# Sinkhorn block attention with a residual MLP on one core: the first token half read from two PSUM tiles, row sums on ScalarE, and batches 2 and 3 mixed half a batch earlier

## The chip, the core and the metric

One core of one Trainium2 chip. The time is the device time in microseconds (us) of one launch: 275.54 us before the change, the median of three runs (274.01, 275.54, 275.88). The five engines that matter run their own instruction streams in order: TensorE (PE in the profile; its weight loads are PEld), VectorE (DVE), ScalarE (ACT), GpSimd (POOL) and SyncE (SP, which here only issues transfers). They meet through semaphores. TensorE accumulates in PSUM; the other operands lie in SBUF.

## What is computed

```python
# q, k, v: (4, 8, 768, 64); sort_net: (4, 8, 8, 8)
P = sort_net
for _ in range(5):                      # Sinkhorn
    P = exp(P - max(P, -1)); P = P / (sum(P, -1) + 1e-9); P = P / (sum(P, -2) + 1e-9)
k_sorted = einsum('bhij,bhjcd->bhicd', P, blocks(k))      # 8 blocks of 96 tokens
v_sorted = einsum('bhij,bhjcd->bhicd', P, blocks(v))
attn = softmax(blocks(q) @ k_sorted^T / 8)                # inside each block of 96
x = (attn @ v_sorted), heads side by side                 # (4, 768, 512)
a1 = alpha1 * x + beta1
u = x + lam * einsum('ts,bsd->btd', w_tok, a1)            # tokens mixed, 768 x 768
a2 = alpha2 * u + beta2
out = u + lam * (relu(a2 @ w_ch1) @ w_ch2)                # 512 -> 2048 -> 512
```

## The kernel before

The kernel works on four batches, each in two halves of 384 tokens. The MLP of a half is the frame: 16 `h_unit`s (four matmuls of 128x384 each, then a Relu on ACT from PSUM into `hTa` or `hTb`), then three token tiles `ch_unit`, each cut into four parts of four matmuls of 128x512. All else is hung between these units: `put(b, hf, kind, n, ...)` files work under a key and `run` emits it after unit n; kind "h" stands for the 16 h units and "c" for the 12 parts. Below, "(1,0) c4" is part 4 of half 0 of batch 1.

PE, DVE, ACT and POOL are wrapped in `Engine` (L55), whose `issue` (L65) keeps instructions in program order; so nearly every profile line says L65, and one has to read by tile names. SP is not wrapped: its transfers (L498, L552, L557, L670, L737, L738) go in an order that the tile scheduler chooses.

PSUM has two rings. `psa` has two buffers of two banks (scores `sc_ps`, attention output `x_ps`, key and value mixing `kmix_ps`, `mix_ps`); `psb` has four buffers of one bank (`h_ps`, `ch_ps`, `tok_ps`, and others). A new tile waits until whoever used that buffer last has been read out.

Batch 0 has a path of its own. k and v are sorted by small matmuls (`k_turn`, `v_mix`); `v_sort(n)` first copies a quarter of v into the layout `VD`, on ACT for n = 0 and 3 and on DVE for 1 and 2. `permute` and `wtok` bring w_tok into `w_tokT` by PE transposes. The first token half does not pass through DRAM: `first_tok(g)` (L616) puts the token product for 128 channels into `tok_ps`, and x transposed plus a rank-1 term (`brow`, `rrow`, the row sums of w_tok) into `turn_ps`; ACT copies the first, scaled, to `tok16`; `first_turn` (L632) adds `tok16` to `turn_ps` by one more matmul with the identity, and ACT makes `a2T` of it. The row sums come from six matmuls with a column of ones (`row_sums`, L586).

For a later batch b these steps run beside the MLP of batch b-1:

- `load_kv`, `load_q` (POOL queue, q0 in the profile): for b = 2 at (0,0) c11, for b = 3 at (1,0) c11.
- `mix_v(b, 0..2)`: three times two matmuls and a DVE copy into `mixed`; `bounce_v` and `back_v` (SP) send that through DRAM (`vscr`) into `Vs`, 96 x 64 rows of 64 half-floats. `mix_k`: three times eight matmuls, and four copies each into `kT`. All of these in half (b-1,0) for b = 2 and 3, from h8 on.
- `q_cross` (L495): six DMA transposes of q on SP, at (b-1,0) h11.
- `score` (8 matmuls, an exp on ACT) and `pv` (8 matmuls, reciprocal and product on DVE, and two more DVE operations, `first_affine`, filed in `late` until `flush`): 8 of each per batch, one per unit, from (b-1,0) c8 to (b-1,1) h11. `tails` then moves 32-row pieces.
- `moe_tok` for the first three token tiles, `moe_cross` (three DMA transposes of `u16` into `uT`, on SP, L670) at (b-1,1) c3, `moe_affine` (DVE makes `a2T` from `uT`) at c7. The first h unit of the next half needs that `a2T`.

```python
    def moe_cross(b, hf):
        uT = uT_of[(b, hf)] = att.tile([128, CT, 384], F16, name="uT", tag="uT", bufs=2)
        for m in range(3):
            nc.sync.dma_start_transpose(
                uT[:, :, m * 128:(m + 1) * 128], u16_of[b][:, 3 * hf + m, :],
            )
```

Of the kernel before, what the change touches and what calls it, by code (L numbers as in the profile page):

```python
# [16 lines left out]
def kernel(  # L17
# [58 lines left out]
    pool = Engine(nc.gpsimd)  # L76

# [83 lines left out]

    W1p = const([128, CT, HID], BF, "W1p")
# [8 lines left out]
    pool.dma_start(lamB[:], moe_lam.partition_broadcast(128))  # L171
    for g in range(4):
        pool.dma_start(W1p[:, :, g * 512:(g + 1) * 512], w1v[:, :, g * 512:(g + 1) * 512])
    brow = att.tile([1, C], F16, name="brow", tag="uT", bufs=2)
    rrow = att.tile([1, 384], F16, name="rrow", tag="uT", bufs=2)
    ones16 = const([128, 1], F16, "ones16")
    pool.memset(ones16[:], 1.0)
# [76 lines left out]
    def v_sort(n, eng):  # L254
        eng(
            VD[:, n * 16:(n + 1) * 16, 0:HB],
            v8[:, :, n * 16:(n + 1) * 16].rearrange("p t d -> p d t"),
        )

# [8 lines left out]
    def q_out(g):  # L268
# [8 lines left out]
        4: [lambda: q_out(1), lambda: q_out(2), lambda: q_out(3), lambda: warm(5)],  # L277
# [155 lines left out]
    def pv_first(g):  # L433
        if g == 0:
            x_of[0] = moep.tile([128, 8, C], F16, name="x128", tag="x128", bufs=2)
            a1_of[0] = moep.tile([128, 8, C], F16, name="a1", tag="a1", bufs=1)
        ps = psa([128, 2, 512], FT, "x_ps")[:, :, 0:480].rearrange("p a (k d) -> p a k d", d=80)
        for i in range(NB):
            for h2 in range(2):
                et = ets[(0, g, i // 4)][:].rearrange("p a i t -> p (a i t)")  # L440
                lo = (4 * h2 + i % 4) * BLK
                w = min(128, 8 * BLK - lo)
                val = Vs[0][:, (2 * g + h2) * NB + i, 0:D + 1]
                if i < 6:
                    pe.matmul(ps[0:w, h2, i, 0:D + 1], et[:, lo:lo + w], val, start=True, stop=True)
                else:
                    for a in range(3):
                        pe.matmul(
                            ps[96:128, h2, 3 * (i - 6) + a, 0:D + 1], et[:, lo + a * 32:lo + (a + 1) * 32], val,
                            start=True, stop=True,  # L450
                        )
        rc = att.tile([128, 2, 6], FT, name="rc", tag="rc", bufs=3)
        dve.reciprocal(rc[:], ps[:, :, :, D])
        dve.tensor_tensor(
            x_of[0][:, 0:NT, g * 128:(g + 1) * 128].rearrange("p k (a d) -> p k a d", a=2),
            ps[:, :, :, 0:D].rearrange("p a k d -> p k a d"),
            rc[:].rearrange("p a k -> p k a").unsqueeze(3).to_broadcast([128, NT, 2, D]), ALU.mult,
        )

    def pv(b, g, hf):  # L460
# [20 lines left out]
        flush()  # L481
# [4 lines left out]
    def flush():  # L486
        while late:
            late.pop()()
# [6 lines left out]
    def q_cross(b, kt):  # L495
        if kt == 0:
            qT_of[b] = att.tile([128, H4, S], F16, name="qT", tag="qT", bufs=1)
        nc.sync.dma_start_transpose(  # L498
# [51 lines left out]
    def bounce_v(b):  # L550
        for th in range(2):
            nc.sync.dma_start(  # L552
                vscr[b, :, th * HB:(th + 1) * HB, :], mixed[b][th * 64:(th + 1) * 64, :, :],
            )

    def back_v(b):
        nc.sync.dma_start(Vs[b % 2][0:BLK, :, 0:D], vscr[b].rearrange("x t d -> t x d"))  # L557
# [4 lines left out]
    def permute(half, eng):  # L562
        wp = wp_of[half] = (moep, att)[half].tile(
            [128, 3, NT, 128], F16, name="wp", tag=("u16", "raw")[half], bufs=(1, 2)[half]
        )
        src = wt16[half]
        eng(wp[:, :, :, 0:96], src[:, :, 0:TAIL].rearrange("p m (k c) -> p m k c", c=96))
        eng(wp[:, :, :, 96:128], src[:, :, TAIL:S].rearrange("p m (k c) -> p m k c", c=32))
# [7 lines left out]
    ab2col = const([128, 4 * CT], FT, "ab2col")  # L576

    def prep_ab2(ps):
        tps = ps([128, 4 * CT], FT, "ab2_ps")
        pe.transpose(tps[:], ab2[:], ident16f[:])  # L580
        act.copy(ab2col[:], tps[:])
        dve.tensor_tensor(
            ab2col[:, 3 * CT:4 * CT], ab2col[:, 2 * CT:3 * CT], ab2col[:, 3 * CT:4 * CT], ALU.mult
        )

    def row_sums(ps):  # L586
        ps = ps([1, 384], FT, "rr_ps")
        for ks in range(NT):
            pe.matmul(ps[:], ones16[:], w_tokT[:, ks, 0:384], start=(ks == 0), stop=(ks == NT - 1))
# [26 lines left out]
    def first_tok(g):  # L616
        c = slice(g * 128, (g + 1) * 128)
        tps, ups = (psb([128, 384], FT, n)[:] for n in ("tok_ps", "turn_ps"))
        for ks in range(NT):
            pe.matmul(  # L620
                tps, x_of[0][:, ks, c], w_tokT[:, ks, 0:384], start=(ks == 0), stop=(ks == NT - 1),
            )
        for m in range(3):
            pe.matmul(
                ups[:, m * 128:(m + 1) * 128], x_of[0][:, m, c], ident16[:],
                start=(m == 0), stop=True, skip_group_check=True,
            )
        pe.matmul(ups, brow[:, c], rrow[:], start=False, stop=True, skip_group_check=True)
        act.activation(tok16[:, g, :], tps, AF.Copy, scale=ab2col[:, 3 * CT + g:3 * CT + g + 1])
        return ups  # L630

    def first_turn(g, ups, eng):  # L632
        pe.matmul(ups, ident16[:], tok16[:, g, :], start=False, stop=True, skip_group_check=True)
        affine(0, 0, g, ups, eng)
# [32 lines left out]
    def moe_cross(b, hf):  # L667
        uT = uT_of[(b, hf)] = att.tile([128, CT, 384], F16, name="uT", tag="uT", bufs=2)
        for m in range(3):
            nc.sync.dma_start_transpose(  # L670
# [31 lines left out]
    def last_out(hT, cps, kk, kt):  # L702
        for n in range(2):
# [11 lines left out]
            nc.sync.dma_start(out[B - 1, kt * 96:(kt + 1) * 96, c], ost[0:96, :])  # L715
# [25 lines left out]
    act_out = nc.sync.dma_start  # L741
# [7 lines left out]
    warm(4)  # L749
    kp0 = k_turn(0, 0, psb)  # L750
# [3 lines left out]
    warm(1)  # L754
# [6 lines left out]
    mix_values(0, psb)  # L761
    k_copy(0, 3, kp3, 0, copy)
    k_copy(0, 3, kp3, 1, act.copy)
    v_sort(0, act.copy)
    v_sort(1, copy)
    score(0, 0, 0, psa)
    score(0, 0, 1, psa)
    warm(3, psb)
    v_mix(0, 0, psb, copy)
    v_mix(0, 1, psb, copy)  # L770
    v_sort(2, copy)
# [3 lines left out]
    v_sort(3, act.copy)  # L775
# [8 lines left out]
    permute(0, copy)  # L784
# [3 lines left out]
    wtok(0, act.copy)  # L788
    wtok(1, act.copy)
    wtok(2, act.copy)  # L790
    score(0, 3, 0, psa)
    pv_first(1)
    wtok(3, act.copy)
    wtok(4, act.copy)
    wtok(5, act.copy)
    score(0, 3, 1, psa)
    permute(1, copy)
    row_sums(psb)
    prep_ab2(psb)
    t0 = first_tok(0)  # L800
    pv_first(2)
    first_turn(0, t0, act)
    t1 = first_tok(1)
    pv_first(3)
    first_turn(1, t1, act)
    t2 = first_tok(2)
    first_turn(2, t2, act)
    t3 = first_tok(3)

# [16 lines left out]
    for ks in range(NT):  # L826
        put(0, 0, "h", ks, lambda ks=ks: prep_wtok(ks, 1, psb, (dve.tensor_copy, act.copy)[ks % 2]))
    for n in range(1, B):
        put(max(n - 2, 0), n > 1, *(("h", 10), ("c", 9))[n > 1], lambda n=n: mix_matrix(n))
# [5 lines left out]
    put(0, 0, "c", 3, lambda: moe_affine(0, 1))  # L835
    for b in range(1, B):
        p = b - 1
        off = 3 if b == 1 else 0
        for n in range(3):
            put(p, 0, "h", (13 if b == 1 else 8) + n, lambda b=b, n=n: mix_v(b, n, dve.tensor_copy))  # L840
        put(p, 0, "h", 15 if b == 1 else 10, lambda b=b: bounce_v(b))
        put(p, 0, "c", 4 if b == 1 else 0, lambda b=b: back_v(b))
        for n in range(3):
            put(
                p, 0, *(("c", 3 + 3 * n) if b == 1 else (("h", 15), ("c", 1), ("c", 4))[n]),
                lambda b=b, n=n: mix_k(b, n, ((act.copy, dve.tensor_copy)[(n + (b > 1)) % 2],) * 4),
            )
        for kt in range(NT if b > 1 else 0):
            put(p, 0, "h", 11, lambda b=b, kt=kt: q_cross(b, kt))
        for g in range(0 if b > 1 else H4):  # L850
            put(p, 0, "c", off + (1, 4, 7, 7)[g], lambda b=b, g=g: q_turn_late(b, g, (dve.tensor_copy, act.copy, dve.tensor_copy, act.copy)[g]))
        if b + 1 < B:
            put(p, 0, "c", 11, lambda b=b: load_kv(b + 1), lambda b=b: load_q(b + 1))
        seq = [("s", 0), ("s", 1), ("s", 2), ("p", 0), ("s", 3), ("p", 1), ("p", 2), ("s", 4), ("p", 3), ("s", 5),
               ("p", 4), ("s", 6), ("p", 5), ("s", 7), ("p", 6), ("p", 7)]
        if b == 1:
            when = [("h", 0), ("h", 1), ("h", 2), ("h", 3), ("h", 4), ("h", 5), ("h", 6), ("h", 7), ("h", 8), ("h", 9),
                    ("h", 10), ("h", 11), ("h", 12), ("h", 13), ("h", 14), ("h", 15)]
        else:
            when = [("c", 8), ("c", 9), ("c", 10), ("c", 10), ("c", 11), ("c", 11), ("h", 0), ("h", 1), ("h", 2), ("h", 3),  # L860
                    ("h", 4), ("h", 5), ("h", 6), ("h", 8), ("h", 9), ("h", 11)]
        for (kind, n), (ph, at_) in zip(seq, when):
            f = (lambda b=b, n=n: score(b, n // 2, n % 2, psa)) if kind == "s" else (lambda b=b, n=n: pv(b, n // 2, n % 2))
            put(p, 1 if ph == "h" else 0, ph, at_, f)
        last = [("h", 12), ("h", 15)][b == 1]
        put(
            p, 1, *last, lambda b=b: tails(a1_of[b], 0, C, dve.tensor_copy),
# [3 lines left out]
        for kt in range(3):  # L871
            put(p, 1, "c", 4 if b == 1 else 3, lambda b=b, kt=kt: moe_tok(b, kt, psb))
        put(p, 1, "c", 4 if b == 1 else 3, lambda b=b: moe_cross(b, 0))
        put(p, 1, "c", 8 if b == 1 else 7, lambda b=b: moe_affine(b, 0))
# [5 lines left out]
    for ci in range(2):  # L880
        for m in range(3):
            h_part(0, 0, m, [ci])
    first_turn(3, t3, act)
    for m in range(3):
        h_part(0, 0, m, [2])
# [44 lines left out]
```

## Time and profile before

The profiled execution took 275.76 us, of which the span on the core is 274.0 us; that is 0.22 us over the median of the three timed runs.

| engine | busy us | share of span | instructions |
|---|---|---|---|
| PE | 260.2 | 95% | 2159 |
| DVE | 169.7 | 62% | 351 |
| ACT | 117.1 | 43% | 219 |
| POOL | 96.4 | 35% | 104 |

The stages follow from the first `h_ps` matmul of each half in the timeline of PE. (0,0) begins at 39.58 us, (0,1) at 72.59, (1,0) at 103.24, (1,1) at 132.94, (2,0) at 163.93, (2,1) at 195.32, (3,0) at 223.76 and (3,1) at 248.40. Half (3,1) holds the MLP alone; (3,0) holds the MLP and 18 token matmuls in 24.64 us.

How to read it: spans of PE overlap, since matmuls are pipelined, so the cost of a group is the distance from its start to the next start. Four h matmuls take 0.65 us in this sense, four `ch_ps` matmuls 0.87, six `tok_ps` matmuls 1.29. The releaser named after an idle time is the one that came last. DMA share over 1 means that packets overlap.

### The profile page before, as it was taken

The numbers are of one execution on the slowest core, as the hardware profiler recorded it, in microseconds if no ns is written. First come the engines' busy times: TensorE is split into PE (matmuls) and PEld (weight loads), VectorE is DVE, ScalarE is ACT, GpSimd is POOL, SyncE is SP. The second block draws the span as 40 slices with busy tenths as digits, with TensorE's granted clock in tenths as the row PEclk, the third lists the DMA queues.
The fourth block names the chain that finished last, engine by engine and source line by source line (L and its number), as shares of the span: only waits on it lengthen the run. The fifth ranks groups of instructions, "written<-read, shape, count | busy, mean of one in ns | idle before, by whom it ended". The sixth has DMA issues, their size and how long they took to land.

```text
span 274.0 us, 5366 instructions
## 1 busy us (share of the span) xinstructions
PE 260.2 (95%) x2159; PEld 140.4 (51%) x2173; DVE 169.7 (62%) x351; ACT 117.1 (43%) x219; POOL 96.4 (35%) x104
## 2 busy tenths in 40 slices
PE   7998899999999999999999969999999999999993
PEld 3466555455556444554455424564465445545552
DVE  5787527896468978576778725586689755121032
ACT  2588547234787002553674002554674004604600
POOL 8647102701472094403560824402200746122000
PEclk9999999999999999999999997999999999999999
DMA  6999999998989942249399952149300223012012
GB/s 103 211 206 193 206 207 214 173 115 178 128 176 175 133 116 78 59 115 145 86 182 165 113 138 61 38 118 117 106 10 2 76 58 77 22 38 77 0 41 77
DMA packets 67372, 31.04 MB, mean 113 GB/s; under 512 B 56642, under 2 KB 63058, under 8 KB 67348
## 3 DMA queue, kind: packets, MB, share of 16 engines
q0 software_dynamic: 26352, 15.34, 40.1%
q1 hardware_dynamic: 40900, 15.30, 30.9%
q8 instruction: 17, 0.28, 0.4%
q14 instruction: 7, 0.06, 0.1%
q10 hardware_dynamic: 96, 0.07, 0.1%
HBM read 32.79 MB, written 8.65 MB: 151 GB/s over the span
## 4 chain that ended last, share of the span: by engine, by line
PE 77%; DVE 9%; DMA 6%; issue 3%; SPq 2%; ACT 2%; POOL 0%; DVEq 0%; POOLq 0%
PE h_ps L65 30%; PE ch_ps L65 21%; PE tok_ps L65 10%; PE x_ps L65 3%; DMA out_dram<-ost 2%; PE sc_ps L65 2%; DVE ost L65 2%; DVE a L65 2%; DVE x L65 2%; PE warm_ps L65 2%; DMA q<-in_q_dram 2%; DMA uT<-u 2%; PE mix_ps L65 1%; PE kmix_ps L65 1%; SPq L737 1%
## 5 line engine op out<-in xcount | busy, mean ns | idle before, releaser
L65 PE MATMUL h_ps<-a2T,W1p 128*128 128x384 bf16 x512 | 97.2, 328 | 2.4 <-DVE a2T L65 2.1
L65 ACT ACTIVATE hTa<-h_ps 128x384 bf16<-128x384 f32 x96 | 47.0, 492 | 95.3 <-PE h_ps L65 95.1
L65 PE MATMUL ch_ps<-W2p,hTa 128*128 128x512 bf16 (+1 forms) x287 | 67.3, 370 | 0.6
L65 POOL TENSOR_TENSOR ost<-ost,u 128x512 f32<-128x512 f32 x21 | 26.6, 1267 | 116.1 <-DVE ost L65 110.0
L65 PEld LDWEIGHTS <-W1p 128*128 128x128 bf16 x512 | 47.6, 99 | 35.3 <-issue 5.0
L65 PEld LDWEIGHTS <-hTa 128*128 128x128 bf16 x300 | 28.4, 98 | 29.0
L65 DVE TENSOR_TENSOR ost<-ch_ps,lamB 128x512 f32<-128x512 f32 (+1 forms) x25 | 16.7, 670 | 37.9 <-PE ch_ps L65 34.6
L65 POOL TENSOR_TENSOR u<-toktmp,x 128x512 f32<-128x512 f32 x18 | 29.2, 1635 | 6.7 <-DVE toktmp L65 6.6
L65 PE MATMUL tok_ps<-a,w_tokT 128*128 128x512 f16 x126 | 30.5, 386 | 0.0
L65 ACT ACTIVATE et<-sc_ps 96x768 f16<-96x768 f32 (+1 forms) x32 | 25.6, 812 | 10.8 <-PE sc_ps L65 10.8
L65 PE MATMUL ch_ps<-W2p,hTb 128*128 128x512 bf16 (+1 forms) x99 | 24.8, 370 | 0.1
L65 DVE TENSOR_TENSOR toktmp<-tok_ps,lamB 128x512 f32<-128x512 f32 x21 | 14.4, 687 | 11.8 <-PE tok_ps L65 10.5
L65 PEld LDWEIGHTS <-w_tokT 128*128 128x128 f16 x126 | 12.3, 99 | 14.5 <-issue 1.1
L65 DVE TENSOR_TENSOR u<-toktmp,x 128x512 f16<-128x512 f32 (+1 forms) x24 | 18.9, 800 | 0.7
L65 ACT ACTIVATE hTb<-h_ps 128x384 bf16<-128x384 f32 x32 | 15.7, 490 | 8.0 <-PE h_ps L65 7.6
L65 POOL DMA_DIRECT2D qn<-in_q_dram x18 | 16.0, 924 | 4.7 <-DMA raw<-in_v_dram 4.7
L65 DVE CAST kT<-kmix_ps 64x512 f16<-64x512 f32 x20 | 14.2, 712 | 4.5 <-PE kmix_ps L65 3.0
L65 DVE TENSOR_TENSOR x<-x_ps,rcb 96x512 f16<-96x512 f32 x24 | 16.5, 686 | 0.8
L65 PE MATMUL x_ps<-Vs,et 96*128 96x65 f16 (+4 forms) x288 | 14.4, 195 | 2.3 <-DVE x L65 1.1
L65 DVE TENSOR_SCALAR a2T<-uT,ab2col 128x384 bf16<-128x384 f16 x28 | 10.6, 440 | 9.3 <-DMA uT<-u 9.3
L65 PEld LDWEIGHTS <-et 96*128 96x128 f16 (+4 forms) x288 | 12.4, 100 | 7.2 <-DVE x L65 2.3
L65 ACT CAST kT<-kmix_ps 64x512 f16<-64x512 f32 x16 | 11.5, 716 | 9.8 <-PE kmix_ps L65 9.6
(113 smaller groups left out, 237.8 us busy)
## 6 DMA issues: line engine op xcount, KB each, us to landing
out_dram<-ost SPq DMA_DIRECT2D x23, 192.0 KB, 2.4
raw<-in_v_dram POOLq DMA_DIRECT2D x6, 384.0 KB, 8.1
raw<-in_k_dram POOLq DMA_DIRECT2D x6, 384.0 KB, 10.0
qn<-in_q_dram POOLq DMA_DIRECT2D x18, 128.0 KB, 10.3
vscr<-mixed SPq DMA_DIRECT2D x6, 384.0 KB, 3.6
Vs<-vscr SPq DMA_DIRECT2D x3, 768.0 KB, 8.0
W1p<-in_moe_w_ch_dram POOLq DMA_DIRECT2D x4, 512.0 KB, 13.0
W2p<-in_moe_w_ch_dram POOLq DMA_DIRECT2D x4, 512.0 KB, 17.3
```

Source lines behind the costliest of these rows:

```text
L65: ins = getattr(self.eng, name)(*args, **kwargs)
L737: act_out(out[b, kt * 96:(kt + 1) * 96, :], ost[0:96, :])
```

## The change

- SP is wrapped too: all transfers on it go in program order.
- The first token half keeps its two PSUM tiles apart. `first_turn` has ACT write alpha2 * (x transposed + rank 1) + beta2 into a new tile `z`; `first_mm` makes `tok_ps`; `first_finish` has DVE compute `a2T = tok_ps * scale + z` in one operation. The identity matmul goes. `tok16` is still copied by ACT. The fourth group is moved behind the first three h matmuls.
- The row sums of w_tok come from ACT (`row_sum`, a copy with `accum_out`, three of 128x768), then three narrow PE transposes.
- `v_sort`: 0 and 1 on DVE, 2 on ACT, 3 on POOL, ahead of the four W1 loads in its queue. `mix_values(0)` is put ahead of `k_turn`. The two small `ab2col` steps go earlier, `permute` is cut, and four of the six first `wtok` copies go from ACT to DVE.
- For b = 2 and 3, `mix_v`, `bounce_v`, `q_cross` and `mix_k` move from half (b-1,0) to the c stage of half (b-2,1), with all copies on ACT; `back_v` goes to (b-1,0) h6; the loads of batch 3 go from (1,0) c11 to (1,0) h6.
- For b = 2 and 3 scores and pv go in pairs, at (b-1,0) h15, c1, c3, c6, c8, c11 and (b-1,1) h1, h4; `flush` is put one unit after each pair of pv. `tails` goes from h12 to h8, the three first `moe_tok` from c3 to c0, c1, c2, `moe_cross` from c3 to c2, `moe_affine` from c7 to c6.

```diff
+    sp = Engine(nc.sync)
...
+    v_sort(3, pool.tensor_copy)
     for g in range(4):
         pool.dma_start(W1p[:, :, g * 512:(g + 1) * 512], w1v[:, :, g * 512:(g + 1) * 512])
...
+    def row_sum(m):
+        if m == 0:
+            a1_of[0] = moep.tile([128, 8, C], F16, name="a1", tag="a1", bufs=1)
+        act.activation(a1_of[0][:].rearrange("p k c -> p (k c)")[:, 0:S], wt16[0][:, m, :], AF.Copy, accum_out=rcol[:, m:m + 1])
...
     def row_sums(ps):
-        ps = ps([1, 384], FT, "rr_ps")
-        for ks in range(NT):
-            pe.matmul(ps[:], ones16[:], w_tokT[:, ks, 0:384], start=(ks == 0), stop=(ks == NT - 1))
+        rc16 = const([128, 3], F16, "rc16")
+        act.copy(rc16[:], rcol[:])
+        ps = ps([1, 384], F16, "rr_ps")
+        for m in range(3):
+            pe.transpose(ps[:, m * 128:(m + 1) * 128], rc16[:, m:m + 1], ident16[:])
         act.copy(rrow[:], ps[:])
...
+    def first_finish(g):
+        dve.scalar_tensor_tensor(
+            a2T_of[0][0][:, g, :], tps_of[g], ab2col[:, 4 * CT + g:4 * CT + g + 1], z_of[0][:, g, :],
+            op0=ALU.mult, op1=ALU.add,
+        )
+        if g == 3:
+            tok_copy(g)
...
-    def first_turn(g, ups, eng):
-        pe.matmul(ups, ident16[:], tok16[:, g, :], start=False, stop=True, skip_group_check=True)
-        affine(0, 0, g, ups, eng)
+        act.activation(
+            z_of[0][:, g, :], ups, AF.Identity, bias=ab2col[:, CT + g:CT + g + 1], scale=ab2col[:, g:g + 1],
+        )
...
+        else:
+            for n in range(3):
+                put(p - 1, 1, "c", 4 + n, lambda b=b, n=n: mix_v(b, n, act.copy))
+                put(p - 1, 1, "c", 7 + 2 * n, lambda b=b, n=n: mix_k(b, n, (act.copy,) * 4))
+            put(p - 1, 1, "c", 7, lambda b=b: bounce_v(b))
+            put(p, 0, "h", 6, lambda b=b: back_v(b))
+            for kt in range(NT):
+                put(p - 1, 1, "c", 6 + kt, lambda b=b, kt=kt: q_cross(b, kt))
+            if b + 1 < B:
+                put(p, 0, "h", 6, lambda b=b: load_kv(b + 1), lambda b=b: load_q(b + 1))
+            for (kind, n), at_ in zip(
+                pairs, ((0, "h", 15), (0, "c", 1), (0, "c", 3), (0, "c", 6), (0, "c", 8), (0, "c", 11), (1, "h", 1), (1, "h", 4)),
+            ):
+                if kind == "p":
+                    put(p, at_[0], at_[1], at_[2] + 1, flush)
+                for i in range(2):
+                    f = (lambda b=b, n=n + i: score(b, n // 2, n % 2, psa)) if kind == "s" else (lambda b=b, n=n + i: pv(b, n // 2, n % 2))
+                    put(p, *at_, f)
...
-            put(p, 1, "c", 4 if b == 1 else 3, lambda b=b, kt=kt: moe_tok(b, kt, psb))
-        put(p, 1, "c", 4 if b == 1 else 3, lambda b=b: moe_cross(b, 0))
-        put(p, 1, "c", 8 if b == 1 else 7, lambda b=b: moe_affine(b, 0))
+            put(p, 1, "c", 4 if b == 1 else kt, lambda b=b, kt=kt: moe_tok(b, kt, psb))
+        put(p, 1, "c", 4 if b == 1 else 2, lambda b=b: moe_cross(b, 0))
+        put(p, 1, "c", 8 if b == 1 else 6, lambda b=b: moe_affine(b, 0))
...
-    for ci in range(2):
+    for m in range(3):
+        h_part(0, 0, m, [0])
+    first_turn(3, psa)
+    first_mm(3, psa)
+    for ci in (1, 2):
         for m in range(3):
             h_part(0, 0, m, [ci])
```

Here `pairs` is `[("s", 0), ("s", 2), ("p", 0), ("s", 4), ("p", 2), ("s", 6), ("p", 4), ("p", 6)]`; `p` is b-1.

## The prediction

> **What bounds the kernel now.** I read the page's engine shares and slices first, then PE by half, then the chain around the one half that is too long, then the queues that feed it.
>
> ```profile
> PE   7998899999999999999999969999999999999993
> ...
> PEclk9999999999999999999999997999999999999999
> ```
>
> ```profile
> 24.14:41.65 17.51, 15.89 (x192) 10.25 (x193) 7.42 (x13) 9.98 (x19) 3.84 (x6) 1.00 1.24 207
> ...
> 72.59:103.24 30.65, 30.41 (x258) 15.66 (x259) 22.75 (x49) 13.84 (x26) 15.84 (x16) 1.00 1.07 145
> 103.24:132.94 29.70, 29.50 (x206) 15.60 (x208) 20.11 (x36) 13.27 (x24) 8.69 (x6) 1.00 0.61 103
> 132.94:163.93 30.99, 28.25 (x215) 14.66 (x213) 21.56 (x47) 10.83 (x21) 15.94 (x16) 1.00 1.04 136
> 163.93:195.32 31.39, 31.19 (x206) 16.09 (x208) 19.72 (x36) 13.27 (x24) 8.77 (x6) 0.95 0.54 93
> 195.32:223.76 28.44, 27.85 (x215) 14.66 (x213) 23.14 (x49) 10.83 (x21) 8.56 (x6) 1.00 0.14 37
> ```
>
> PE is full in nearly every slice: it is the bound, and only PE work removed or PE stalls closed can shorten the span. The windows (length, then busy us of PE, PEld, DVE, ACT, POOL, then clock, DMA share and GB/s) show where PE is not full: 1.6 us before the first h units, 2.7 us in (1,1); and (2,0) ran at a granted clock of 0.95. The chain of waits there:
>
> ```profile
> 158.93 0.83 SPq L670
> ...
> 161.16 2.32 DMA uT<-u
> ...
> 163.50 0.39 DVE a2T L65
> ...
> 163.93 1.19 PE h_ps L65 x4
> 165.13 2.11 PE tok_ps L65 x6
> 167.23 2.17 PE h_ps L65 x8
> ```
>
> PE waits 2.05 us for `a2T`, that for `uT`, that for SP. Then the next groups are slow: 1.19, 2.27 and 2.38 us in the timeline where 0.81, 1.46 and 1.46 are usual, 2.1 us lost, at a granted clock of 0.60 from 164.8 to 168.2. The SP queue says why `uT` was late, and two more rows price what the change moves:
>
> ```profile
> 122.45 0.34 SPq L557 DMA_DIRECT2D Vs<-vscr  x1
> ...
> 148.86 8.20 SPq L498 DMA_TRANSPOSE qT<-qn  x6
> ...
> 158.25 4.13 SPq L670 DMA_TRANSPOSE uT<-u  x3
> ```
>
> ```profile
> 137.34 0.34 PE L65 MATMUL sc_ps<-qT,kT 64*128 64x96 f16 x8
> 137.62 0.82 PE L65 MATMUL h_ps<-a2T,W1p 128*128 128x384 bf16 x4
> 138.28 0.42 PE L65 MATMUL x_ps<-Vs,et 96*128 96x65 f16 x8
> 138.54 0.82 PE L65 MATMUL h_ps<-a2T,W1p 128*128 128x384 bf16 x4
> ```
>
> Six q transposes hold SP from 148.86 to 157.16, an output and then `uT` follow. From starts: a score costs 0.28 us, a pv 0.26; but from an h start to the next score is 0.75 and to the next pv 0.66, so a switch into scores costs about 0.10 more.
>
> **The change up to the first h units, before 41.65 us.** There the fourth weight slice of h units 0 to 2 begins. PE loses four identity matmuls (0.17 each, 0.66) and six row-sum matmuls (29.70 to 30.76, 1.06, less some 0.25 for three narrow transposes): 1.5 us in all. Following each engine in order with these rows: VD waits for DVE now, whose three `bigV` steps (0.22 each) and two small ones push the k copies back by 0.75, so v_mix starts at about 18.1 as before; its seventh copy is ACT's, so attention output begins at 24.0 (was 24.14). v_sort(3) on POOL is not in the trace: between 0.4 (its 256-element copy) and 1.5 us (ACT's); even 3 us would end by 20, v_mix needs it at 22. It holds up W1 (issued 16.8, landing 13 us later, needed at 39.6): hidden by 10 us. From 24.0: x_ps and scores as before, DVE takes four w_tokT copies (0.36) and two halves of `permute` (1.4), so the third x is ready at 32.3, the fourth at 34.7; the token product 0 ends at 31, 2 at 35; the fourth after the first h slice, at 37.4; its `first_finish`, priced at 0.6 by the 512-wide product from PSUM (0.69) and bounded by 0.44 and 0.96, at 38.15; slice four begins at 38.4. The three ACT row sums cost 0.8 each by the exp of the same width; at 1.5 (the strided copy) `rrow` is 1.5 us late and the first turn waits for it. So 41.65 becomes 38.4, or 39.9: gain 3.25, at worst 1.7. The later (0,0) has one 0.13 matmul more (`mix_matrix(2)`): gain 3.1. Its loads stay ahead: queue q0 finishes q of batch 1 at 57, needed at 64.
>
> **The halves from 72.59 to 223.76.** These last 151.2 us. What PE has to do there, from starts: MLP 20.76 (16 x 0.65 + 12 x 0.865) and tokens 3.88 in each of five halves; mixing 2.65 (3 x 0.43 + 3 x 0.45). After the change:
>
> - (0,1): 30.65, less 0.13 and the 0.25 wait, and 2.65 of mixing: 32.9.
> - (1,0): 24.64, four score pairs (2 x 0.27 + 0.10 = 0.64, so 2.56), four pv (1.04), 0.13: 28.4.
> - (1,1): 24.64, four pv, 2.65: 28.3. (2,0): 28.2. (2,1): 25.7.
>
> Sum 143.5: 7.7 us less. Of these 4.2 are the wait at 163.93 and its clock, 0.8 the pairs, about 1.1 two waits for DVE's x (136.33, 198.61), the rest smaller waits. This holds if `uT` comes in time: three tokens at c0 to c2, the last u16 about 8.2 us into the stage, `uT` 2.5 us later, DVE 1.25: ready at 12; the stage runs for 17. q's transposes now stand behind `uT` on SP.
>
> What is added against that:
>
> 1. *ACT's queue.* Each mix_k costs ACT four copies, 2.9 us; three are issued within 4.4 us, so 8.7 us of copies reach past the stage. The end of the third is some 4.4 us into the next half. Behind it on ACT are the Relus; `psb` has four buffers, so the second token group (PE ready 3.25 us in) waits for the first Relu at 4.8. PE waits 1.6 us at (1,0) and at (2,0): 3.2. Below, 0, if the third mix_k gets its copies sooner than these rows say; above, what rival B adds.
> 2. *Vs.* back_v stands on SP behind the three `uT` of (b-1,0) h4. From the end of the third token group T: product 0.96, u16 0.73, transpose 1.2, so it is issued at T + 2.95 and lands 8.0 later (all three landings took 8.0): T + 11.0. The first pv pair needs it after 11 h units, two score pairs and four ch parts: T + 11.9. For batch 3 that is enough. For batch 2 POOL issues the loads of batch 3 at about T + 2.6 to 4.7, on the same 16 engines. No row shows the two together. Vs is 6144 packets of 128 B, which filled 122.5 to 129.0; k and v are 256 packets of 6144 B at 474 ns, and q 6144 small ones. Below: nothing lost. Above: Vs moves one small packet per big one, gets through only after k and v (8 us) and then shares with q: 11.5 us of waiting. I take the time shared equally: in the row of batch 2's load only 39 of 256 packets moved in the first 3 us, so Vs, which moved 1710 in its first 1.5 us alone, gets about 2900 out early; the other 3200, 3.3 us alone, take 6.6, then 1.5 to be seen: T + 13.9, PE waits 2.0 us. Behind it on PE stands everything. A clock drop after it costs 0 (waits of 0.59 and 0.81 had none) to 1.7 (after 2.05): as 2.0 stands at the edge, 0.85.
>
> The Trainium skill ("DMA: Bandwidth & Descriptors", section on queues, rings and completion order) says that an engine takes rows in turn by the packet, some 9 to 17 descriptors at a time. By that rule, an estimate, sixteen small ones (0.27 us) would alternate with a 0.47 us one, Vs would come some 5 us late, and with a clock drop the sum be about 274.7. No run here shows it yet.
>
> SP's order otherwise: outputs of c7 now stand between q's first transpose and the rest; `ost` has two buffers, so a late output stops DVE only a tile later, and none is that late by my count: 0.
>
> Sum: -3.1 - 7.65 + 3.2 + 2.0 + 0.85 = -4.7. Against the profiled 275.76 that is 271.06; the profiled run was 0.22 above the median, so 270.8.
>
> **Rivals.**
>
> A. *Vs behind the loads*, at the first pv pair of (1,0). For: back_v and the loads are issued within half a microsecond, and the margin is 0.9. Against: Vs starts first. Without any Vs term the sum is 268.0; a wait of 6 to 11.5 us and a clock drop of 1.7 give 275.7 to 281.2. From a wait of 8.6 us on it is over 1% slower.
>
> B. *ACT becomes the bound at two h starts*, with a clock drop each: 3.4 more, 274.2. For: ACT gets 12 copies and 3 more per batch. Against: 1.6 us is less than the 2.05 that had a drop.
>
> C. *The front does not get shorter*: DVE (34.7 for the last x) or ACT takes the place of PE, or POOL's copy is several us. 273.9.
>
> D. Nothing of the Vs and ACT waits appears: 264.8.
>
> **How the numbers follow.** The forecast with its near cases (267 to 273, D included) has 0.64; A 0.18, B 0.09, C 0.09. 1% (272.8 to 278.3) is about what a measurement can tell here. Faster: 0.61 of the forecast, 0.04 of B and C: 0.65. Slower: half of A and a little: 0.10. Same: 0.25. Range: from 265.5, near D, to 276.5, which leaves out most of A. The forecast's own range is 267 to 273.
>
> **What would show it.** First h slice four at 38.4 (C: over 41). No `h_ps <- DVE a2T` wait and a PEclk without the dip at 164. Stage lengths as listed. PE waiting for ACT at the second token group of (1,0) and (2,0), under 2 us each. At the first pv of (1,0), PE waiting for DMA Vs: about 2 us, in A over 6, with Vs landing in 15 us or more while q0 moves big packets. Wrong would be: pairs that wait for their exps in the c stage (I count 0.3 us of slack), an SP queue where `uT` is late behind an output, or DVE's flushes coming before an `ost` that PE needs.

## The result, and the profile after

The changed kernel takes 285.29 us (median of four runs, 284.43 to 285.87) where the kernel before, run beside it, takes 274.77 (273.17 to 275.88): a ratio of 1.0385, 95% interval 1.0317 to 1.0453. It is slower, and outside the range that was given. The profiled execution took 284.78 us, its span is 283.0.

Two rows of the page of the changed kernel, and its halves, cut at the first `h_ps` matmul of each half as before (length, then busy us of PE, PEld, DVE, ACT, POOL, then clock, DMA share, GB/s):

```profile
PE   8988999999999997960599999799999999999993
...
PEclk9999999999999999996599999999999999999999
```

```profile
70.67:103.47 32.80, 32.64 (x287) 17.55 (x288) 23.89 (x52) 20.94 (x35) 16.02 (x17) 1.00 0.86 125
103.47:148.93 45.46, 30.59 (x228) 15.71 (x228) 14.87 (x35) 16.56 (x30) 16.20 (x16) 0.85 0.91 126
148.93:177.25 28.32, 28.21 (x194) 15.65 (x193) 16.47 (x37) 16.25 (x27) 8.76 (x6) 1.00 0.25 52
177.25:207.08 29.83, 27.95 (x226) 14.82 (x226) 13.45 (x29) 16.53 (x29) 8.79 (x6) 1.00 0.67 111
207.08:232.77 25.69, 25.59 (x164) 13.77 (x163) 16.20 (x36) 9.14 (x18) 8.76 (x6) 1.00 0.16 37
```

The dip at 164 us is gone, and a far larger one stands in the slices around 120 to 142 us. One half carries all of it:

| stretch | before | predicted | after |
|---|---|---|---|
| up to (0,1) | 72.59 | 69.5 | 70.67 |
| (0,1) | 30.65 | 32.9 | 32.80 |
| (1,0) | 29.70 | 32.85 with the Vs terms, 30.0 without | 45.46 |
| (1,1) | 30.99 | 28.3 | 28.32 |
| (2,0) | 31.39 | 29.8 with the wait for ACT | 29.83 |
| (2,1) | 28.44 | 25.7 | 25.69 |
| the rest | 50.24 | 50.24 | 50.23 |

PE's waits of the changed kernel (who waited for whom: us in total, times, longest), and the chain of waits through (1,0) (start, length, what):

```profile
PE x_ps L65 <- DMA Vs<-vscr: 12.8, 1, 12.8
PE tok_ps L65 <- ACT hTa L65: 3.5, 2, 1.7
```

```profile
115.43 1.22 SPq L65
...
116.70 20.59 DMA Vs<-vscr
...
137.42 1.09 PE x_ps L65 x16
```

Vs took 20.59 us from issue to landing where each of its three landings took 8.0 before. The queues of SP and POOL at that point show the two issues side by side:

```profile
112.81 3.83 SPq L65 DMA_TRANSPOSE uT<-u  x3
116.70 0.90 SPq L65 DMA_DIRECT2D Vs<-vscr  x1
```

```profile
115.16 1.10 POOL L65 DMA_DIRECT2D raw<-in_v_dram  x2
116.25 1.06 POOL L65 DMA_DIRECT2D raw<-in_k_dram  x2
117.26 4.46 POOL L65 DMA_DIRECT2D qn<-in_q_dram  x5
```

The trace has each packet with its queue (q0 is POOL's, q1 SP's), its size and its start. Counted per us in the changed kernel, on the time axis of the rows above:

```
us       q0: 6144 B   q0: 128 B   q1: 256 B (uT)   q1: 128 B (Vs)
118          23            -            -                -
119          13            -          217                -
120          27            -          295                -
122          33            -            -               41
123          32            -            -               37
126           -          530            -              541
130           -          571            -              563
134           -          569            -              566
```

While k and v are moving, about one packet of Vs, 128 bytes, goes for each packet of 6144; while q is moving, one small packet for one small packet. That is the upper bound of the prediction, not the value taken. The packets of `uT`, just ahead of Vs on the same queue, do not go by such turns: from 119.52 to 120.63 us, 512 of them went beside 18 big ones.

The clock behind the wait (windows of the changed kernel, columns as above):

```profile
124.60:128.20 3.60, 0.02 (x1) 0.00 (x0) 0.82 (x2) 0.00 (x0) 1.43 (x2) 1.00 1.57 157
128.20:137.40 9.20, 0.00 (x0) 0.01 (x1) 0.00 (x0) 0.00 (x0) 0.00 (x0) 0.54 1.95 161
137.40:141.90 4.50, 4.26 (x24) 2.23 (x26) 3.20 (x8) 0.00 (x0) 0.00 (x0) 0.50 0.02 6
141.90:145.00 3.10, 3.10 (x28) 1.31 (x26) 0.38 (x1) 1.50 (x2) 0.00 (x0) 0.89 0.00 0
```

The means of 0.54 and 0.89 hold a change each; the trace's clock records put the half clock from 128.90 to 142.55 us. So it begins 4.3 us after PE stopped and lasts 5.15 us after PE starts again, which costs about 2.5. With that, (1,0) is 28.4 of work, 1.7 of waiting for ACT, 12.8 for Vs and about 2.5 of clock: 45.4 of 45.46.

### The profile page after: what moved, and what is told of

It is laid out like the page before. It is cut to its first block, busy times and chain, and to the rows that moved or that the text cites. A ratio compares the mean times of both kernels' runs of the same rounds, so it can differ in the third digit from the quotient of the medians.

```text
span 283.0 us, 5356 instructions
## 1 busy us (share of the span) xinstructions
PE 256.9 (91%) x2149; PEld 140.3 (50%) x2165; DVE 153.3 (54%) x341; ACT 133.5 (47%) x242; POOL 99.2 (35%) x104
## 4 chain that ended last, share of the span: by engine, by line
PE 77%; DMA 8%; ACT 6%; DVE 5%; issue 2%; SPq 1%; DVEq 0%
PE ch_ps L65 25%; PE h_ps L65 25%; PE tok_ps L65 10%; DMA Vs<-vscr 7%; ACT kT L65 6%; PE x_ps L65 4%; PE warm_ps L65 4%; PE sc_ps L65 2%; DVE a L65 1%; PE v_ps L65 1%; PE mix_ps L65 1%; SPq L65 1%; PE kmix_ps L65 1%; DVE ost L65 1%; DMA out_dram<-ost 1%
## 5 line engine op out<-in xcount | busy, mean ns | idle before, releaser
L65 PE MATMUL h_ps<-a2T,W1p 128*128 128x384 bf16 x512 | 91.9, 326 | 0.0
L65 ACT ACTIVATE hTa<-h_ps 128x384 bf16<-128x384 f32 x96 | 46.3, 493 | 53.0 <-PE h_ps L65 52.9
L65 PE MATMUL ch_ps<-W2p,hTa 128*128 128x512 bf16 (+1 forms) x287 | 70.0, 378 | 0.9 <-issue 0.2
L65 PE MATMUL x_ps<-Vs,et 96*128 96x65 f16 (+4 forms) x288 | 13.4, 198 | 13.9 <-DMA Vs<-vscr 12.8
L65 ACT CAST kT<-kmix_ps 64x512 f16<-64x512 f32 x32 | 22.9, 715 | 6.2 <-PE kmix_ps L65 5.9
L65 PE MATMUL ch_ps<-W2p,hTb 128*128 128x512 bf16 (+1 forms) x97 | 24.2, 370 | 0.2
L65 DVE TENSOR_SCALAR a2T<-uT,ab2col 128x384 bf16<-128x384 f16 x28 | 9.9, 418 | 15.4 <-DMA uT<-u 15.4
L65 DVE TENSOR_TENSOR u<-toktmp,x 128x512 f16<-128x512 f32 (+1 forms) x24 | 17.4, 735 | 0.7
L65 DVE RECIPROCAL rcb<-x_ps 96x8 f32<-96x8 f32 x24 | 4.8, 198 | 20.4 <-PE x_ps L65 20.4
```

Source lines behind the costliest of these rows:

```text
L65: ins = getattr(self.eng, name)(*args, **kwargs)
```

## The experiments

**Loads of batch 3 back to where they were.** On the changed kernel:

```diff
-                put(p, 0, "h", 6, lambda b=b: load_kv(b + 1), lambda b=b: load_q(b + 1))
+                put(p, 0, "c", 11, lambda b=b: load_kv(b + 1), lambda b=b: load_q(b + 1))
```

> The changed kernel with one edit: the loads of batch 3 go back from (1,0) h6 to (1,0) c11, so that nothing else is on the transfer engines while Vs of batch 2 comes in. Theory (Vs shares the engines packet by packet with those loads, one of its 128-byte packets for each of theirs): Vs lands in about 8.0 us instead of 20.6, PE waits under 0.5 us for it, half (1,0) takes about 30.0 us instead of 45.46, the run about 285.3 - 12.8 - 2.2 = 270 us. Rival (SP in program order issues back_v too late, or the exps hold up the pairs): (1,0) stays over 40 us and the run over 280.

270.87 us, ratio to the kernel before 0.9833 (0.9775 to 0.9891). Vs lands in 7.9 us, (1,0) takes 30.46. One line of the diff decides the sign. The theory holds: neither SP's order nor the pairs hold up (1,0). PE still waits a little for Vs:

```profile
125.66 0.67 PE L65 MATMUL x_ps<-Vs,et 96*128 96x65 f16 x16 [0.27 <-DMA Vs<-vscr]
```

**The same collision in the kernel before.** On the kernel before, for b = 2 only:

```diff
-            put(p, 0, "c", 11, lambda b=b: load_kv(b + 1), lambda b=b: load_q(b + 1))
+            put(p, 0, *(("c", 11) if b == 1 else ("h", 15)), lambda b=b: load_kv(b + 1), lambda b=b: load_q(b + 1))
```

> The kernel before with one edit: the loads of batch 3 go from (1,0) c11 to (1,0) h15, so that they are under way when Vs of batch 2 is issued (122.45 us in the profile of before). Theory: Vs takes 18 us or more to land, the pv at (1,0) c10 waits for it for 8 to 12 us and the clock drops after it, so that the run is 283 to 290 us. Rival (the harm needs the order of SP or the pairs of the changed kernel): Vs lands within 12 us, the wait is under 2, the run under 278.

284.43 us. Vs takes 17.1 us (a little under the 18 expected; its v load had gone through earlier), and PE waits 11.9 for it:

```profile
143.16 0.63 PE L65 MATMUL x_ps<-Vs,et 96*128 96x65 f16 x8 [11.86 <-DMA Vs<-vscr]
```

So the harm needs nothing else of the change: the overlap of the two transfers is enough. The turns are not there from the first packet on: here Vs got 1307 packets out from 129.32 to 131 us, while 26 of k's started, and only then went one for one, 32 for 31 in the us from 131.

**Which loads, and by what rule.** On the changed kernel, k and v alone early, and q alone early:

```diff
-                put(p, 0, "h", 6, lambda b=b: load_kv(b + 1), lambda b=b: load_q(b + 1))
+                put(p, 0, "h", 6, lambda b=b: load_kv(b + 1))      # second run: load_q
+                put(p, 0, "c", 11, lambda b=b: load_q(b + 1))      # second run: load_kv
```

> The changed kernel with only k and v of batch 3 (256 packets of 6144 bytes) at (1,0) h6, its q at (1,0) c11. Theory, packet for packet: until k and v are through, at about 125 us, Vs gets through some 35 packets per us; then it has the engines alone at some 950 per us, 6.2 us for the rest: it lands at about 132.5, PE waits about 8 us, the run takes about 280 us. Rival (equal shares of the engines' time): Vs lands at about 129, PE waits 4, the run about 275.

> The changed kernel with only q of batch 3 (6144 packets of 128 bytes) at (1,0) h6, its k and v at (1,0) c11. Theory, packet for packet: small packets against small ones, both at about 565 per us, so Vs takes about 11 us of moving and lands at about 129.5, PE waits about 5 us, the run takes 275 to 278 us. Rival (equal shares of the engines' time): the same here as with k and v early, so the two runs would be alike.

281.02 and 277.29 us. Vs lands in 15.8 and 13.2 us; one row of PE from each, k and v early first:

```profile
133.30 1.09 PE L65 MATMUL x_ps<-Vs,et 96*128 96x65 f16 x16 [8.10 <-DMA Vs<-vscr]
```

```profile
130.03 1.09 PE L65 MATMUL x_ps<-Vs,et 96*128 96x65 f16 x16 [5.38 <-DMA Vs<-vscr]
```

About 8 and 5 us were expected by counting packets, 4 in both by equal time. The packets agree: with k and v, 34 of Vs for 33 of the loads in the us from 125, then 1027 to 1136 per us alone; with q, 571 for 557 in the us from 124. Once both are moving, Vs and the loads take turns by packet, nearly one for one, whatever its size.

The Trainium skill ("DMA: Bandwidth & Descriptors", section on queues, rings and completion order) has an engine drain some 9 to 17 descriptors of one queue before it goes to the next. The runs show turns, but of one packet of the trace each; the estimate by that rule, about 5 us late, was well under the 12.8 measured. On this point the measurement decides.

**v_sort on POOL.** The front gained 1.9 us instead of 3.1. In the changed kernel DVE's sort copy and POOL's, from DVE's and POOL's timelines:

```profile
16.69 1.81 DVE L65 COPY vd<-v 128x768 f16<-128x768 f16 x1
...
18.89 0.81 DVE L65 COPY vd<-v 128x768 f16<-128x768 f16 x1
```

```profile
16.33 1.49 POOL L65 COPY vd<-v 128x768 f16<-128x768 f16 x1 [0.44 <-DMA v<-in_v_dram]
```

The first DVE copy starts while POOL copies and ends 0.68 us after POOL does. Two runs, both on the loads-late kernel: the fourth `v_sort` on ACT, and on POOL behind the second W1 load.

```diff
-    v_sort(3, pool.tensor_copy)                 # ahead of the W1 loads
...
+    v_sort(3, act.copy)                         # first run: after v_mix(0, 3)
+        if g == 1: v_sort(3, pool.tensor_copy)  # second run: in the loop of W1 loads
```

> The loads-late kernel with the fourth quarter of v sorted on ACT again (after the fourth v_mix) instead of on POOL. In the loads-late profile DVE's first sort copy ran from 17.04 to 18.72 us, 1.68 long, while POOL's copy of the same form ran from 16.53 to 18.03; DVE's second one, alone, took 0.82. Theory (POOL's copy holds up DVE's): DVE's first copy takes about 0.8, the first v_mix with a sorted v starts about 0.75 us earlier relative to the k copies. Rival (the first copy is long for another reason, its source just landed or a cold read): it stays at 1.7.

> The loads-late kernel with POOL's sort copy behind its second W1 load instead of ahead of the first. Theory (the two copies collide): DVE's first sort copy takes about 0.8, POOL's then runs beside DVE's casts from PSUM (0.62 each), which keep their time if only copies from SBUF collide, and get about 1 us longer in all if every DVE operation does. Start of the first h unit about 0.7 us earlier than with the copy ahead, if nothing else takes the place. Rival: DVE's first copy stays at 1.7.

270.75 and 271.94 us in one run each, which says nothing at this size; the rows do. DVE's copy takes 0.81 in both. In the second run POOL's copy stands beside three casts from PSUM, which take 1.88 together, as they do without it (1.87):

```profile
16.80 0.81 DVE L65 COPY vd<-v 128x768 f16<-128x768 f16 x1
...
18.73 1.88 DVE L65 CAST Vs<-v_ps 128x512 f16<-128x512 f32 x3
```

```profile
19.50 1.51 POOL L65 COPY vd<-v 128x768 f16<-128x768 f16 x1
```

So DVE's copy from SBUF is held while POOL's runs, and the casts from PSUM do not mind. "SBUF — State Buffer" of the Trainium skill (section on who interferes with whom) calls the ports that the two engines share an exclusive lock; these rows agree for this copy.

The first h unit began at 36.64 with ACT and at 37.45 with POOL later, against 37.24 in the loads-late kernel. That is no gain that can be told: the nine profiles with POOL's copy ahead, the changed kernel's among them, range from 36.26 to 37.24. A gap of PE for which the profile names no releaser takes the place, always after the thirteenth matmul of the same v_mix. In those nine it lasts from nothing to 1.01 us; in the three profiles with the copy moved (one is of a run further on) 1.24, 1.79 and 1.94. PE's row behind it in the changed kernel and with ACT:

```profile
22.07 0.47 PE L65 MATMUL v_ps<-bigV,vd 64*64 64x64 f16 x19 [0.46 <-issue]
```

```profile
21.79 0.47 PE L65 MATMUL v_ps<-bigV,vd 64*64 64x64 f16 x19 [1.24 <-issue]
```

The trace points to its cause. Queue q8 carries packets of 16384 bytes that the trace calls `instruction`. One of them ends 1.2 to 1.5 us before the gap does in each of the thirteen profiles of this case that have the gap, the kernel before included (at 20.64 us in the changed kernel, 20.52 with ACT). With q early it ended at 20.44, and there was no gap. The 0.81 us gap at 28.27 us in the kernel before follows such a packet by 1.37 too. So PE seems to wait there for its next piece of program, and work that is ready sooner waits longer; no run moves that packet alone.

**ACT's queue, and where its wait goes.** The third mix_k's copies on DVE, on the loads-late kernel:

```diff
-                put(p - 1, 1, "c", 7 + 2 * n, lambda b=b, n=n: mix_k(b, n, (act.copy,) * 4))
+                put(p - 1, 1, "c", 7 + 2 * n, lambda b=b, n=n: mix_k(b, n, ((act.copy, act.copy, dve.tensor_copy)[n],) * 4))
```

> The loads-late kernel with the four copies of the third mix_k of batches 2 and 3 on DVE instead of ACT. Theory (ACT's queue holds the first Relu and so a PSUM buffer): the waits of PE for the Relu at the second token group of (1,0) and (2,0), 1.75 and 1.72 us, go, both halves take about 28.7 us, the run takes 3 to 3.5 us less than with loads late, about 267.5. Rival (DVE becomes the late one): PE waits for DVE's toktmp or ost in the same place, and the run stays within 1 us of 270.9.

273.31 us in one run: nothing gained. Both waits for the Relu are gone, and PE waits for Vs instead, 2.31 us in (1,0), with half the clock for 3.41 us behind it, and 2.96 in (2,0):

```profile
125.56 0.67 PE L65 MATMUL x_ps<-Vs,et 96*128 96x65 f16 x16 [2.31 <-DMA Vs<-vscr]
...
186.57 0.69 PE L65 MATMUL x_ps<-Vs,et 96*128 96x65 f16 x16 [2.96 <-DMA Vs<-vscr]
```

Vs was issued at 117.35 us, in the loads-late kernel at 117.61: SP's queue sets that time, and PE now arrives earlier and waits longer. (The expectation of the run with both edits, further on, puts it down to DVE's later u16; that reading was wrong, since u16 was done at 112.83 and SP took up `uT` at 113.46, after q's last transpose.)

**SP in the scheduler's order.** On the loads-late kernel:

```diff
-    sp = Engine(nc.sync)
+    sp = nc.sync
```

> The loads-late kernel with SP's transfers in the order of the scheduler again: it puts all six q transposes ahead of the uT ones and of the output, and Vs ahead of the second half's uT. Theory (it was the move of moe_cross to c2 and not SP's order that closed the 2.05 us wait at the head of (2,0)): no wait for a2T comes back, Vs is issued earlier, the run is within 1 us of 270.9. Rival (the order is what closed it): PE waits 1 us or more for a2T at the start of (2,0), with the clock drop behind it, and the run is 272.5 or more.

273.28 us in one run, and the theory fell. SP's and PE's rows of this run:

```profile
150.41 5.55 SPq L519 DMA_TRANSPOSE qT<-qn  x4
156.05 1.22 SPq L712 DMA_TRANSPOSE uT<-u  x1
157.37 3.89 SPq L519 DMA_TRANSPOSE qT<-qn  x2
161.35 2.54 SPq L712 DMA_TRANSPOSE uT<-u  x2
```

```profile
165.66 1.19 PE L65 MATMUL h_ps<-a2T,W1p 128*128 128x384 bf16 x4 [3.48 <-DVE a2T L65]
```

q's transposes stand ahead of and between those of `u`, and the wait at the head of (2,0) is back, longer than before the change. So the earlier `moe_cross` alone does not close it: the program order on SP is needed. Whether that order is enough with `moe_cross` left at c3 was not run.

**Vs ahead of uT, and then the rest.** On the loads-late kernel: back_v from h6 to h3; that and the third mix_k on DVE; both and v_sort on ACT.

```diff
-            put(p, 0, "h", 6, lambda b=b: back_v(b))
+            put(p, 0, "h", 3, lambda b=b: back_v(b))
```

> The loads-late kernel with back_v at (1,0) and (2,0) h3, so that Vs goes ahead of the three uT transposes on SP. Theory (what is left of the wait for Vs is its place behind uT): PE's waits for Vs (0.27 and 0.54 us) go, the waits for the Relu (1.75, 1.72) stay, the run takes about 0.8 less than with loads late, 270. Rival (the wait is only handed on): uT, now behind 768 KB on the same queue, comes late, DVE stands at moe_affine with pv's work behind it, and PE waits 1 us or more for DVE in the c stage or at the next half.

> back_v at h3 and the third mix_k's copies on DVE together, on the loads-late kernel. Theory (with the copies on DVE alone the wait moved from the Relu to Vs, because DVE's later u16 held up uT and so back_v behind it): with Vs ahead of uT neither wait is left, halves (1,0) and (2,0) take about 28.6 us each, the run about 270.9 - 3.5 - 0.8 = 266.6. Rival (DVE's delay goes on to something else): the halves stay over 30, the run over 269.

> The same with the fourth v_sort on ACT. Theory: DVE's sort copy takes 0.8 instead of 1.7, but PE's gap at about 22 us, for which the profile names no releaser, ends at the same time as before and takes most of that back: 0 to 0.7 us less than with back_v and mix_k alone, about 266.3; against the kernel before a ratio of about 0.967. Rival (ACT's fourth copy holds up its exps): 0.5 us or more slower than without it.

269.73 us in one run; 270.52 (ratio to the kernel before 0.9842, 0.9789 to 0.9895); 269.23 (0.9794, 0.9742 to 0.9847); 270, 266.6 and 266.3 were expected. The first does what was expected: no wait for Vs, both waits for ACT, (1,0) in 30.0 us. In the second the wait went on once more, the rival's way. DVE's and PE's rows of it:

```profile
125.80 1.25 DVE L65 TENSOR_SCALAR a2T<-uT,ab2col 128x384 bf16<-128x384 f16 x4 [7.73 <-DMA uT<-u]
```

```profile
128.54 0.34 PE L65 MATMUL sc_ps<-qT,kT 64*128 64x96 f16 x8 [2.12 <-DVE x L65]
129.37 0.34 PE L65 MATMUL sc_ps<-qT,kT 64*128 64x96 f16 x8 [0.49 <-DVE x L65]
```

DVE, in program order, stands at `moe_affine` for a `uT` that comes behind Vs, and the attention work that PE needs is queued behind it. In the third the gap near 22 us was 1.94 us in the profiled run, with a clock drop after it; its six runs spread from 268.31 to 271.03.

**The last one moved.** On the second of these:

```diff
-        put(b, 0, "h", 13, lambda b=b: moe_affine(b, 1))
+        put(b, 0, *(("h", 13) if b == B - 1 else ("c", 5)), lambda b=b: moe_affine(b, 1))
```

> back_v at h3 and the third mix_k's copies on DVE, as in the run of both, and moe_affine of the second half of batches 1 and 2 at c5 instead of h13. In the run of both, DVE stood 7.73 us at moe_affine for uT, which came behind Vs, with the pv work behind it, and PE waited 2.12, 0.49, 0.87 and 0.49 us for x before scores. Theory (that place in DVE's order is all that is left): these waits go, (1,0) takes about 28.6 and (2,0) about 28.5 us instead of 30.98 and 29.48, the run about 267.2, ratio about 0.971. Rival (the wait is handed on again): a2T comes late for the first h unit of (1,1) or (2,1), PE waits there, and the run stays over 269.5.

266.20 us (265.24 to 266.84), ratio to the kernel before 0.9675, interval 0.9629 to 0.9722: faster than both kernels. What is left of waits of PE past the front:

```profile
PE x_ps L65 <- DMA Vs<-vscr: 0.7, 1, 0.7
```

(1,0) takes 28.11 us and (2,0) 28.78.

## Why the prediction was wrong

- **The step that failed** is the second of the two added waits: "I take the time shared equally ... so Vs ... gets about 2900 out early", T + 13.9, a wait of 2.0 us. Measured, with T, the end of the third token group, at 112.51 us: a landing at T + 24.8, a wait of 12.8. Nothing of Vs got out early: its first packet moved at 122.12 us, 5.7 us after the loads' first. Vs was issued at T + 4.2 instead of T + 2.95, since SP, at q's last transpose until 112.73 us, then spent 3.83 us on three `uT` transposes in a row, where the sum counted one, 1.2. Then the third `uT`, issued at 115.43, stood ahead of it on the same queue, and its packets did not move before 119.52; what held them back is not shown. From there on Vs took about one turn per packet of the loads. The end that the prediction called "above" (11.5 us) was the right one, and its mechanism was too. Shown by the run that takes the overlap away, the one that puts it into the kernel before, and the two that split it. (Counted from each transfer's first packet, the 39 and 1710 packets behind the 2900 are 54 and 1956, which alters nothing here.)
- **Rival A** had the place, the price (275.7 to 281.2 against 285.3) and the sign; it was given 0.18. It came out higher for 1.3 us more of waiting than its upper end, 0.8 more of clock and 1.2 less gain in the front.
- **The clock** after it: at most 1.7 was allowed; 5.15 us at half speed cost about 2.5. By the trace's clock records it was halved for 13.65 us here, and in the two runs with part of the loads for 10.24 us (wait 8.1) and 6.83 us (wait 5.4), in each from 3.1 to 4.3 us into the wait on. An edge at a wait of 2 us, on which the 0.85 rests, does not show: a wait of 2.31 us had a drop behind it, but waits of 2.12 (both edits) and 2.96 us (the copies on DVE) had none. The price itself, 1.7, fits its row: before, at 164 us, the records have half the clock for 3.41 us. The 2.1 us that the prediction reads there hold 0.4 of the first h group, which takes 1.19 us at the head of (1,0) too, without a drop.
- **The halves** were right: 32.9, 28.3, 29.8 and 25.7 predicted, 32.80, 28.32, 29.83 and 25.69 measured. Pairs, mixing ahead and the closed wait for `a2T` gave what the sum said.
- **The wait for ACT** was right in place and size: 1.6 predicted at each of two heads, 1.74 and 1.72 measured, and both went with the copies.
- **SP's program order** was priced at nothing, and the closing of the 2.05 us wait was put down to earlier tokens and `moe_cross`, with q's transposes behind `uT`. That place behind `uT` is the order's work, and the closing needs it (3.48 us come back without it).
- **The front** was off in size: slice four began at 39.47 (predicted 38.4), and (0,1) 1.92 us earlier than before (predicted 3.1). It was late already at the first attention output, 25.00 us for 24.0. The term that is shown mis-sized is DVE's first sort copy, 1.81 us for 0.81 alone: POOL's copy was priced by its own length (1.49, inside the bounds), and not by what it does to DVE beside it. But in the runs that give that us back the first h unit began no earlier than in the others, so the copy alone does not account for the miss; the gap near 22 us, which the sum left out, stands beside it. `first_finish` took 0.62 (0.6 taken) and a row sum 0.83 (0.8 taken).

## What to carry to other kernels

In these runs a transfer of many small packets gave about one turn to each packet of the load beside it, however long that packet was, and so waited for nearly all of the load; before a load is moved, ask which latency-bound transfer it will share the engines with, and price that at the upper end. Where both ends of an unknown are worked out and the margin behind them is under a microsecond, let the sum show the far end as a case of its own size. A wait taken out in a chain of queues comes back at the next queue in order: here Relu, Vs, uT, x. With the copies and `back_v` moved the time stayed at 270.52 us (270.87 without); only with `moe_affine` moved too did it fall to 266.20.

## What was not expected of the hardware

- One-for-one turns of the two transfer queues, even between 128 and 6144 bytes: 41 and 37 packets of Vs in the us from 122 and 123, against 33 and 32 of the loads. `uT`'s packets took no such turns (512 beside 18).
- A copy from SBUF on DVE waits for one on POOL: 0.81 alone, 1.81 beside it, while casts from PSUM keep their 0.62.
- A gap of PE of 0.2 to 1.9 us at the same instruction near 22 us in thirteen of fourteen profiles (two matmuls later in the kernel before), longest where the work ahead of it was fastest. It ends 1.2 to 1.5 us after a packet of instructions does; that PE waits for its program there is inferred from that alone.
